# A written-out instruction plan, refitted with measured durations of VectorE, ScalarE and the first GpSimd transfer

## The chip, the core and the metric

The kernel runs on one core of a Trainium2 chip. The metric is the device time of one execution in microseconds. The kernel before takes 267.25 us (median of three runs, 267.24 to 267.47). The profiled execution took 267.04 us; its span, from the first to the last instruction of the program, is 265.3 us, and all times of the profile count from the start of that span.

## What is computed

Sparse attention, and behind it a feed-forward block with a squared relu. Queries, keys and values have 4 batches, 8 heads, 768 rows and 64 columns. The keys are cut into 24 chunks of 32. For each query an upper bound of its score with each chunk comes from the chunk's smallest and largest key in each column; the six chunks with the largest bounds, among those not in the future, are kept.

```python
k_min = np.min(k_chunks, axis=3)
k_max = np.max(k_chunks, axis=3)
ub = np.sum(np.maximum(q[:, :, :, None, :] * k_min[:, :, None, :, :], q[:, :, :, None, :] * k_max[:, :, None, :, :]), axis=-1)
...
top_chunks = np.argsort(ub, axis=-1)[..., -top_k:]
...
scores = np.where(mask, scores, -1000000000.0)
...
attn = np.exp(scores)
attn = attn / (np.sum(attn, axis=-1, keepdims=True) + 1e-09)
return np.matmul(attn, v).astype(np.float32)
...
h = np.maximum(x @ w_in, 0.0)
return (h * h @ w_out).astype(np.float32)
```

The feed-forward block has 3072 tokens, 512 columns and an inner width of 2048.

## The kernel before

**Tiling.** Rows are cut into tiles of 128, six for each batch. The first tile of each batch attends only to itself and needs no selection; it has a path of its own (`first_transposes` L541, `first_attention` L554). The other five tiles of a batch are done for two heads at a time: 16 pairs p = 0 to 15, four for each batch. `stage_a` (L620) prepares a pair: it transposes keys and queries (kT, qT), reduces the keys to the chunks' largest and smallest (kr, L688), forms the positive and negative part of the queries (qp, qm, L704), multiplies for the bounds (ub, L654), adds the causal mask (ubm, L713), finds the top six with max (m8, L662) and compares (selb, L718). The transposed selection is copied into 24 extra rows of the queries (qsc), and the extra rows of the keys hold a large negative number, so that one matmul gives scores with the selection already in them. `stage_b` (L757) computes for each head five banks of scores (ps, L773), the exps on ScalarE (e, L795), a triangular mask on the diagonal blocks (`causal`, L747: on VectorE as a product with tri, L750, or on GpSimd as an affine select, L753) and the product with the values (av, L784). `normalise` (L599) divides by the row sum.

**Feed-forward.** `ffn` (L814) is called once for the four first tiles together and once for the five other tiles of each batch. It transposes x (xt, xT), multiplies with w_in (ph, `up`, L857), takes the relu (ht, on ScalarE L864 or VectorE L866), squares it on VectorE (h, L875), and multiplies with w_out (py, `down`, L888); a copy (ob, L274 or L276) and a store follow.

**Transfers.** GpSimd issues most loads (L361, L439, L446, L426 and the weights, L453 and L459), which turn float32 into bf16. SyncE issues four loads of first tiles (L391), the transposes by DMA of batches 2 and 3 (L381) and the stores.

**The plan.** None of the orders is written by hand. Every operation is a `plan.op` with a cost on each engine that could do it, a due time, and what it needs. `Plan.order` (L112) plays these operations through: it keeps a time at which each engine is free, times at which each buffer comes free, and a small model of the transfers (`Transfers`, L42), always starts what can start first, and among what can start at about the same time on one engine takes the least due time (L157). Where two engines can do an operation, the one that could start it first gets it. `write` (L192) then emits the instructions in the order of these start times. So the costs and due times decide both the order on each engine and which engine does a mask, a copy or a relu. When TensorE is expected to be idle early on, `keep_warm` (L517) fills the gap with matmuls on a constant tile, which no one reads.

The due times come from the table `P` (L234): `lead` says how long before its pair's scores each preparation is due, `va` and `vm` how long after the scores the value product and the mask are due, `f_due` when the first tiles' attention is due, `up_due`, `up_rate`, `due` and `rate` when the feed-forward steps are due, `ra` and `h2` when relu and square are due, `loads` and `later` the order of the transfers.

Of the kernel before, what the change touches and what calls it, by code (L numbers as in the profile page):

```python
# [13 lines left out]
ACT = mybir.ActivationFunctionType  # L14
# [27 lines left out]
class Transfers:  # L42


    RATE = 1 / 0.00083
    FIRST = 600

    def __init__(self):
        self.now = 0.0
# [17 lines left out]
    def add(self, op):  # L67
# [3 lines left out]
        if not op.turns and not self.begun:  # L71
            self.begun = True
            work += self.FIRST
        self.queues[op.turns].append([op, work])
# [3 lines left out]
class Plan:  # L78
# [7 lines left out]
    HAND_OVER = {"PE": 0.22, "ACT": 0.10, "DVE": 0.10, "POOL": 0.12, "SP": 0.1}  # L86
    BUSY = 0.09
    WARM = 8.0
    FILL = 26.0
    NEVER = 1e9  # L90

# [6 lines left out]

    def op(self, where, due, fn, needs=(), tiles=(), packets=0, turns=False,
           late=0.0):  # L100
        op = Op(where, due, fn, [n for n in needs if n is not None],
                [t for t in tiles if t is not None], packets, turns)
        for t in op.tiles:
            t.users.append(op)
        op.late = late
        op.number = -1 if packets and not turns else len(self.ops) - len(self.loads)
        self.ops.append(op)
        if packets and not turns:
            self.loads.append(op)
        return op  # L110

    def order(self):  # L112
        free = {e: 0.7 for e in ("PE", "ACT", "DVE", "POOL", "SP")}
        slots = {tag: [0.0] * n for tag, n in self.slots.items()}
        waiting = {}
        count = {}
        for op in self.ops:
            for t in op.tiles:
                t.left = len(t.users)
            count[op] = len(op.needs)  # L120
            for n in op.needs:
                waiting.setdefault(n, []).append(op)
        ready = [op for op in self.ops if not count[op]]
        landed, done = [], []
        dma = Transfers()
        while ready:
            found = []
            for op in ready:
                if op.packets and not op.turns and op is not self.loads[len(landed)]:
                    continue  # L130
                at = 0.0
                new = {}
                for t in op.tiles:
                    if not t.held:
                        new[t.tag] = new.get(t.tag, 0) + 1
                for tag, n in new.items():
                    at = max(at, sorted(slots[tag])[n - 1]
                             if n <= len(slots[tag]) else self.NEVER)
                if at == self.NEVER:
                    continue  # L140
                if op.packets and not op.turns and len(landed) >= 8:
                    at = max(at, landed[-8].end)
                for engine, cost in op.where.items():
                    st = max(at, free[engine])
                    for n in op.needs:
                        same = n.engine == engine and not n.packets
                        lag = (0.0 if engine == "PE" else self.BUSY) if same                             else self.HAND_OVER[n.engine]
                        st = max(st, n.end + lag)
                    for t in op.tiles:
                        if t.psum:  # L150
                            for e, end in t.last.items():
                                if e != engine and "PE" not in (e, engine):
                                    st = max(st, end + self.HAND_OVER[e])
                    found.append((st, op, engine, cost))
            assert found, "nothing can start"
            first = min(found, key=lambda f: (f[0], f[1].number))
            st, op, engine, cost = min(  # L157
                (f for f in found if f[2] == first[2] and f[0] <= first[0] + self.wait),
                key=lambda f: (f[1].due, f[0], f[1].number))
            ready.remove(op)  # L160
            if engine == "PE":
                op.fill = 0
                fresh = [t for t in op.tiles if t.psum]
                if st < self.FILL and fresh and not any(t.held for t in fresh):
                    room = max([free[engine]] + [sorted(slots[t.tag])[0] for t in fresh])
                    op.fill = max(0, int((st - room - 0.3) / 0.216))
                if st < self.WARM:
                    cost *= 2
            op.engine, op.start, op.end = engine, st, st + cost
            free[engine] = op.end  # L170
            if op.packets:
                dma.add(op)
                if not op.turns:
                    landed.append(op)
            for t in op.tiles:
                if not t.held:
                    t.held = True
                    slots[t.tag].remove(min(slots[t.tag]))
                t.last[engine] = max(t.last.get(engine, 0.0), op.end)
                t.left -= 1  # L180
                if not t.left:
                    slots[t.tag].append(
                        max(u.end + self.HAND_OVER[u.engine] for u in t.users))
            for n in waiting.get(op, ()):
                count[n] -= 1
                if not count[n]:
                    ready.append(n)
            done.append(op)
        assert len(done) == len(self.ops), "operations left"
        return sorted(done, key=lambda op: op.start)  # L190
# [12 lines left out]
def kernel(  # L203
# [27 lines left out]
    QC = 128 * NS  # L231
    VW = 80
    NSET = 4
    P = dict(lead=[26, 15, 48, 47, 26, 61, 5, 53, 70, 14, 26, 79, 70, 28, 8, 54],  # L234
             f_due=[207, -206, -290.97, -438.97], sp='K0 Q0 K1 Q1', rows=-1719,
             rows_after=0, up_due=-34.03, up_rate=11.93, half=4,
             due=[-21, -128, -27, -2], rate=[4.44, 7.05, 5.27, 4.28], va=11.75,
             vm=13.01, ra=0.57, h2=-0.91, later='k1 q1 v1 k2 q2 q3 v2 k3 v3', shift={},
             p0=-7210, wait=0.01,
             loads="k0 q0 V2 Q3 V1 K3 K2 V0 Q2 k1 V3 "  # L240
                   "i0 q1 v0 i3 i2 v1 k2 R2 q2 i1 o0 q3 k3 o1 v2 v3 o2 o3")

    nc.scalar.preload_act_table_set("natural_log_exp_and_others")

# [15 lines left out]
                 "vn": B - 1, "x": 2, "xT": 2,  # L260
                 "kr": 2, "qp": 2, "qm": 2, "ubm": 2, "m8": 2, "rc": 2}, lambda *a: keep_warm(*a), P["wait"])
    POOLS = {"tp": pst, "ps": pss, "av": psav, "ff": psf, "e": epool, "h2": hpool,
# [148 lines left out]
    def ones(b, due):  # L411
        def go(engine):
            e = nc.vector if engine == "DVE" else nc.gpsimd
            e.memset(nat["v", b].tile[:, :, :, D:D + 1].rearrange(
                "p j h o -> p (j h) o"), 1.0)

        made["ones", b] = plan.op({"DVE": 0.12, "POOL": 0.3}, due, go,
                                  tiles=[nat["v", b]])
# [52 lines left out]

    for i, what in enumerate(P["sp"].split()):
        if what[0].isupper():
# [8 lines left out]
    made["ubmask"] = plan.op({"DVE": 0.8}, -997, make_ubmask)  # L482
    for what in P["loads"].split():
        i = int(what[1])
# [11 lines left out]
    for b in range(1, B):  # L496
        ones(b, 20 * NP * b - 70)
    for what in P["later"].split():
        nm, b = what[0], int(what[1])
# [17 lines left out]
    def keep_warm(dst, n):  # L517

        size = 1
        for dim in dst.shape[1:]:  # L520
            size *= dim
        dst = dst if len(dst.shape) == 2 else dst.rearrange(
            {3: "p a b -> p (a b)", 4: "p a b c -> p (a b c)"}[len(dst.shape)])
        if dst.dtype == F32:
            size = min(size, 512) // 128 * 128 or size
            for _ in range(n * 512 // size):
                nc.tensor.matmul(
                    dst[:, 0:size].rearrange("p (a b) -> p a b", b=min(size, 128)),
                    lhsT=warm, rhs=warm[:, 0:min(size, 128)].unsqueeze(1).to_broadcast(
                        [128, size // min(size, 128), min(size, 128)]),  # L530
                    start=True, stop=True)
        else:
            for _ in range(4 * n):
                transpose(dst[:, 0:128], warm)
# [19 lines left out]
    def first_attention(b, tags, due):  # L554
# [30 lines left out]
        for hh in range(2):  # L585
# [5 lines left out]
                        [es[hh], av[hh]])  # L591
            if (b, hh) == (0, P["rows_after"]):
                rows([e])
# [15 lines left out]
    def rows(after):  # L609
        made["rows", 0] = plan.op({"ACT": 0.84}, P["rows"], lambda _: kq_rows(0),  # L610
                                  [made["ident"]] + after)
# [297 lines left out]
    for b in range(B):  # L909
        due = P["f_due"][b]  # L910
# [74 lines left out]
```

The softmax here doesn't subtract the row's maximum and nothing guards it: scores larger than these inputs give would overflow.

## Time and profile before

| engine | busy us | share of 265.3 us | instructions |
|---|---|---|---|
| TensorE, matmuls | 252.9 | 95% | 2378 |
| TensorE, weight loads | 163.9 | 62% | 2403 |
| VectorE | 198.0 | 75% | 699 |
| ScalarE | 180.0 | 68% | 366 |
| GpSimd | 102.9 | 39% | 177 |

A row of a group names the line, the engine, the operation and what it writes and reads, then how often it occurs, its busy time and the mean duration of one in ns, then the idle time of the engine just ahead of it and what ended that. A row of waits names who waited for whom, the sum of these waits, how many there were and the longest. Engines are PE (TensorE), PEld (its weight loads), DVE (VectorE), ACT (ScalarE), POOL (GpSimd) and SP (SyncE). The time of a matmul's row runs from its start to a modelled end, so that rows of matmuls that follow closely overlap.

In 40 slices of the span, TensorE's busy share is 0.9 or more from the seventh slice on to the last but one; VectorE's is 0.9 in most slices between 13 and 150 us and falls off after 210 us; the granted TensorE clock is below full speed only in the first slices.

### The profile page before, as it was taken

Reading aid. Unit: us, or ns where it says so; the run is one execution under the profiler, and the core shown is the slowest. Engines: PE = TensorE matmul, PEld = TensorE weight load, DVE = VectorE, ACT = ScalarE, POOL = GpSimd, SP = SyncE. Lnnn points to the kernel's source line nnn. Section 1 sums busy time; section 2 is a strip of 40 time slices with the busy share of each in tenths; the row PEclk is TensorE's granted clock in tenths of the full one; section 3 lists DMA queues with packets and bytes.
Section 4 is the critical chain, followed back from the end, with each engine's and each line's share of the span. In section 5 each row is a group of like instructions: output and inputs, shape, how many; then the busy total and the mean of one; then the engine's idle time right before and its main releaser. Section 6 shows DMA issues by size and latency. Waiting matters only on the chain.

```text
span 265.3 us, 6528 instructions
## 1 busy us (share of the span) xinstructions
PE 252.9 (95%) x2378; PEld 163.9 (62%) x2403; DVE 198.0 (75%) x699; ACT 180.0 (68%) x366; POOL 102.9 (39%) x177
## 2 busy tenths in 40 slices
PE   6789989999999999999999999999999999999995
PEld 2556755666677666566686556567766666465443
DVE  6689999978999999999998898677877543255000
ACT  1779669855599898769697949667889532376112
POOL 8997756887404837757340112011101000000000
PEclk9689999999999999999999999999999999999999
DMA  9999999999982999999990010263000020200222
GB/s 142 167 177 184 173 171 121 163 155 200 186 138 40 94 129 114 162 140 141 114 249 4 0 53 5 68 129 96 17 0 2 1 80 1 79 4 0 79 82 79
DMA packets 103733, 26.12 MB, mean 98 GB/s; under 512 B 96332, under 2 KB 100708, under 8 KB 103700
## 3 DMA queue, kind: packets, MB, share of 16 engines
q0 software_dynamic: 75168, 13.33, 66.3%
q1 hardware_dynamic: 28532, 12.36, 21.6%
q8 instruction: 19, 0.31, 0.5%
q14 instruction: 14, 0.11, 0.2%
HBM read 27.26 MB, written 6.29 MB: 126 GB/s over the span
## 4 chain that ended last, share of the span: by engine, by line
PE 74%; DVE 11%; ACT 6%; POOL 3%; DMA 2%; issue 2%; SPq 1%; ACTq 0%; DVEq 0%
PE py L888 27%; PE ph L857 25%; PE ps L773 10%; PE av L784 6%; DMA raw<-in_q_dram 2%; DVE h L875 2%; ACT qsc L274 2%; POOL vn L439 2%; DVE kr L688 1%; ACT ht L864 1%; DVE qsc L276 1%; DVE m L662 1%; DVE kqc L276 1%; PE xt L279 1%; PE T L279 1%
## 5 line engine op out<-in xcount | busy, mean ns | idle before, releaser
L857 PE MATMUL ph<-xT,w_in_sb 128*128 128x256 bf16 (+2 forms) x592 | 96.4, 304 | 2.1 <-ACT ht L864 1.2
L795 ACT ACTIVATE e<-ps 128x512 bf16<-128x512 f32 x160 | 87.0, 608 | 9.7 <-PE ps L773 7.4
L888 PE MATMUL py<-w_out_sb,h 128*128 128x512 bf16 (+2 forms) x375 | 88.8, 370 | 1.2
L857 PEld LDWEIGHTS <-w_in_sb 128*128 128x128 bf16 x592 | 56.2, 97 | 27.1 <-issue 4.5
L864 ACT ACTIVATE ht<-ph 128x384 bf16<-128x384 f32 (+2 forms) x120 | 53.6, 452 | 19.5 <-PE ph L857 15.9
L753 POOL TENSOR_SCALAR_AFFINE_SELECT e<-e 128x128 bf16<-128x128 bf16 (+1 forms) x82 | 27.8, 342 | 93.9 <-ACT e L795 84.9
L875 DVE TENSOR_TENSOR h<-ht 128x256 bf16<-128x256 bf16 (+2 forms) x148 | 46.8, 330 | 19.9 <-ACT ht L864 13.1
L888 PEld LDWEIGHTS <-h 128*128 128x128 bf16 x400 | 36.0, 97 | 32.2
L773 PE MATMUL ps<-qsc,kqc 88*128 88x128 bf16 (+1 forms) x320 | 53.2, 272 | 0.1
L274 ACT COPY ob<-py 128x512 f32<-128x512 f32 (+2 forms) x23 | 13.1, 569 | 41.4 <-PE py L888 41.4
L784 PEld LDWEIGHTS <-e 128*128 128x128 bf16 x640 | 33.5, 97 | 10.4 <-POOL e L753 0.5
L784 PE MATMUL av<-vn,e 128*128 128x65 bf16 x480 | 34.2, 193 | 0.1
L773 PEld LDWEIGHTS <-kqc 88*128 88x128 bf16 x320 | 25.5, 97 | 10.0 <-issue 0.4
L604 DVE TENSOR_TENSOR x<-av,rc 128x320 bf16<-128x320 f32 (+1 forms) x40 | 18.8, 472 | 0.5
L750 DVE TENSOR_TENSOR e<-e,tri 128x128 bf16<-128x128 bf16 (+1 forms) x46 | 10.3, 232 | 8.1 <-ACT e L795 7.4
L662 DVE MAX8 m<-ubm 128x8 f32<-128x24 f32 x160 | 15.6, 167 | 0.1
L688 DVE TENSOR_REDUCE kr<-kt 128x24 bf16<-128x768 bf16 x16 | 14.9, 945 | 0.1
L688 DVE TENSOR_REDUCE kr<-kT 128x24 bf16<-128x768 bf16 x16 | 14.8, 949 | 0.1
L784 PE MATMUL av<-v,e 128*128 128x65 bf16 x160 | 14.6, 193 | 0.0
L866 DVE TENSOR_SCALAR ht<-ph 128x256 bf16<-128x256 f32 (+2 forms) x28 | 13.3, 480 | 1.5 <-PE ph L857 1.1
L439 POOL DMA_DIRECT2D vn<-in_v_dram x15 | 13.2, 891 | 0.5 <-issue 0.5
L274 ACT COPY qsc<-sT 24x256 bf16<-24x256 bf16 (+1 forms) x29 | 12.5, 432 | 1.1 <-PE sT L279 0.5
(89 smaller groups left out, 247.7 us busy)
## 6 DMA issues: line engine op xcount, KB each, us to landing
out_dram<-ob SPq DMA_DIRECT2D x23, 256.0 KB, 2.4
w_in_sb<-in_moe_w_in_dram POOLq DMA_DIRECT2D x4, 512.0 KB, 7.7
w_out_sb<-in_moe_w_out_dram POOLq DMA_DIRECT2D x4, 512.0 KB, 8.8
vn<-in_v_dram POOLq DMA_DIRECT2D x15, 128.0 KB, 7.0
nt<-in_k_dram POOLq DMA_DIRECT2D x10, 128.0 KB, 6.1
nt<-in_q_dram POOLq DMA_DIRECT2D x10, 128.0 KB, 5.0
kn<-in_k_dram POOLq DMA_DIRECT2D x8, 80.0 KB, 6.6
qn<-in_q_dram POOLq DMA_DIRECT2D x8, 80.0 KB, 7.1
```

What stands on the lines that cost most here:

```text
L274: nc.scalar.copy(dst, src)
L439: load((nm, b), lambda _: nc.gpsimd.dma_start(out=nat[nm, b].tile[:, j - 1, :, 0:D], in_=SRC[nm][b, :, 128 * j:128 * (j + 1)].rearrange("h ...
L604: return plan.op({"DVE": 0.06 + 0.00108 * D * n}, due, lambda _: nc.vector.tensor_mul(x(), av[:, :, 0:D], rc[:, 0:n].unsqueeze(2).to_broad ...
L688: nc.vector.tensor_reduce(kr[:, mm].rearrange("d (t c) -> d t c", c=128 // CH) if b >= BY_DMA else kr[:, mm], part(kT).rearrange("d t (c j ...
L753: nc.gpsimd.affine_select(out=e, in_=e, compare_op=ALU.is_ge, fill=0.0, base=0, channel_multiplier=-1, pattern=[[0, n], [1, 128]])
L773: nc.tensor.matmul(ps[:, 128 * c:128 * (c + nt)], lhsT=kqs[:, s, hh, 128 * j:128 * (j + 1)], rhs=qss[:, s, hh, 128 * (t0 - 1):128 * (t0 - ...
L784: nc.tensor.matmul(av[:, t - 1], lhsT=e[:, 128 * c:128 * (c + 1)], rhs=value_tile(b, h, j), start=(i == 0 and c == 0), stop=(i == len(BANK ...
L795: nc.scalar.activation(e.tile, ps.tile, ACT.Exp, scale=scale), [sc], [ps, e])
L857: nc.tensor.matmul(ph.tile, lhsT=w_in_sb[:, ki, 128 * f:128 * (f + 1)], rhs=xT[:, c0 // 128:c1 // 128, ki], start=(ki == 0), stop=(ki == N ...
L864: nc.scalar.activation(ht.tile, ph.tile, ACT.Relu)
L875: {"DVE": 0.067 + w / 1920}, at[0] + P["h2"], lambda _: nc.vector.tensor_mul(h2[f][:, c0:c1], ht.tile, ht.tile), [op], [ht, h2[f]])))
L888: nc.tensor.matmul(py.tile, lhsT=h2[f][:, 128 * t:128 * (t + 1)], rhs=w_out_sb[:, f, c0:c1], start=(f == 0), stop=(f == NFI - 1))
```

## The change

The planner's durations are made longer, to what was measured, and all orders are fitted again to the new durations. Four edits do it: the first GpSimd transfer costs 1400 packets more than its size instead of 600 (`FIRST`); each cost on ScalarE is multiplied by 1.04 and each on VectorE by 1.05 (`SLOWER`); due times that are equal up to rounding count as equal, so that the earlier start decides; and the table `P` is replaced. No operation of the computation, no buffer and no matmul shape is changed.

```diff
     RATE = 1 / 0.00083
-    FIRST = 600
+    FIRST = 1400
...
     WARM = 8.0
+    SLOWER = {"ACT": 1.04, "DVE": 1.05}
...
            late=0.0):
+        where = {e: c * self.SLOWER.get(e, 1.0) for e, c in where.items()}
         op = Op(where, due, fn, [n for n in needs if n is not None],
...
-                key=lambda f: (f[1].due, f[0], f[1].number))
+                key=lambda f: (round(f[1].due, 6), f[0], f[1].number))
...
-    P = dict(lead=[26, 15, 48, 47, 26, 61, 5, 53, 70, 14, 26, 79, 70, 28, 8, 54],
-             f_due=[207, -206, -290.97, -438.97], sp='K0 Q0 K1 Q1', rows=-1719,
-             rows_after=0, up_due=-34.03, up_rate=11.93, half=4,
-             due=[-21, -128, -27, -2], rate=[4.44, 7.05, 5.27, 4.28], va=11.75,
-             vm=13.01, ra=0.57, h2=-0.91, later='k1 q1 v1 k2 q2 q3 v2 k3 v3', shift={},
-             p0=-7210, wait=0.01,
-             loads="k0 q0 V2 Q3 V1 K3 K2 V0 Q2 k1 V3 "
-                   "i0 q1 v0 i3 i2 v1 k2 R2 q2 i1 o0 q3 k3 o1 v2 v3 o2 o3")
+    P = dict(lead=[29, 46, 59, 39, 24, 71, 13, 53, 78, 15, 28, 72, 60, 6, 47, 77],
+             f_due=[165, -158, -474.97, -240.97], sp='K0 Q0 K1 Q1', rows=-1719,
+             rows_after=0, up_due=-70.08, up_rate=7.25, half=4,
+             due=[-19, -136, -15, 35], rate=[4.42, 7.43, 6.24, 5.06], va=12.05,
+             vm=6.24, ra=0.55, h2=-1.49, later='k1 q1 v1 k2 q2 q3 v2 v3 k3', shift={},
+             p0=-3220, wait=0.01,
+             loads="Q3 k0 K3 q0 V0 V1 V2 K2 Q2 k1 i0 "
+                   "V3 i3 q1 v0 i2 k2 v1 R2 q2 i1 v2 o0 q3 k3 o1 v3 o2 o3")
```

In `loads`, a capital letter with a batch is the first tile of that batch, a small letter with a number is a pair of heads of batch 0, i and o are quarters of w_in and w_out, and R2 copies the extra key rows to the other sets.

## The prediction

> **What bounds the kernel now.** I read the page first, then the windows, the waits and the groups by shape. The page's first part says that no engine but TensorE is near full over the whole span:
>
> ```profile
> PE 252.9 (95%) x2378; PEld 163.9 (62%) x2403; DVE 198.0 (75%) x699; ACT 180.0 (68%) x366; POOL 102.9 (39%) x177
> ```
>
> An average over 265 us hides the stages, so I cut the span at the first up matmul (22.5 us), where VectorE stops being full (about 152), and at the last matmul (261). The columns are stretch, its length, then the busy time of each engine (its instructions):
>
> ```profile
> core 0: us, PE busy (x) PEld busy (x) DVE busy (x) ACT busy (x) POOL busy (x), PEclk, DMA share, GB/s
> 0.00:22.50 22.50, 17.09 (x171) 10.79 (x172) 16.88 (x66) 13.39 (x24) 20.45 (x31) 0.85 1.74 161
> 22.50:152.00 129.50, 126.24 (x1300) 84.60 (x1311) 121.51 (x426) 102.47 (x211) 72.96 (x119) 1.00 1.38 134
> 152.00:261.00 109.00, 108.29 (x894) 67.56 (x905) 59.60 (x209) 63.34 (x132) 9.52 (x28) 1.00 0.15 45
> 261.00:265.30 4.30, 1.28 (x19) 0.98 (x16) 0.00 (x0) 0.74 (x2) 0.00 (x0) 1.00 0.18 62
> ```
>
> TensorE looks full in both long stages, but a busy matmul row includes its latency. I therefore counted columns: each weight load of the trace is paired with its matmul in the program's order, and a column costs 1/2.4 ns (two 512-column matmuls of the last stage start 216 ns apart, 1% more than this rate). That gives 10.6, 119.2, 105.8 and 0.9 us of streaming in the four stretches, 236.5 us in all. So 11.9 us are lost in the start, 10.3 in the middle, 3.2 in the third stage and 3.4 in the tail. The third stage streams 97% of its time; the middle streams 92%, and there VectorE is busy 121.5 of 129.5 us (94%), ScalarE 79%, GpSimd 56%. In the middle two engines are nearly full together, and neither has room to wait for the other. Who waits for whom over the whole run:
>
> ```profile
> POOL e L753 <- ACT e L795: 84.9, 69, 9.3
> ...
> ACT ht L864 <- PE ph L857: 15.9, 44, 1.5
> DVE h L875 <- ACT ht L864: 13.1, 35, 1.6
> ...
> DVE e L750 <- ACT e L795: 7.4, 17, 1.3
> ...
> PEld L784 <- POOL e L753: 0.5, 2, 0.3
> ```
>
> GpSimd's masks wait for exps far more than anything waits for GpSimd: its 82 masks are held up 84.9 us in total, while the value matmuls (L784) waited 0.5 us for them. Here GpSimd is a spare engine for masks and VectorE is not.
>
> **What the Trainium skill says.** "Perfetto Trace Analysis", Identifying the Most-Contended Engine: matmul busy share is no measure of the distance to the limit, occupancy is a fair one for VectorE. The trace agrees: 126 us busy against 119 streamed. "TensorE: Matmul & The Clock Gate", Part 1: the clock falls to half after an idle window of about 3.4 us and returns after a busy one; its Part 4 says that transposes do not count as busy in the same way. The trace shows clock 0.50 from 8.2 to 15.0 us, two such windows, with mostly transposes in the first. "SBUF — State Buffer", Who interferes with whom: VectorE instructions with two SBUF inputs and GpSimd ones that read SBUF block each other. GpSimd's masks took 282 to 1093 ns with a median of 292, so here this is rare.
>
> **The change part by part.** No matmul of the result, no exp and no transfer is added or taken away; the planner (L112) only gets other costs, and it puts the same operations on other engines and places. Comparing the built orders by engine gives this.
>
> 1. Masks: the 128x128 masks on VectorE (L750) fall from 38 to 18, on GpSimd (L753) they rise from 58 to 78. Of the first 32 masks of pairs 0 to 3, VectorE had 25 and gets 9.
>
> ```profile
> L750 DVE TENSOR_TENSOR e<-e,tri 128x128 bf16<-128x128 bf16 x38 | 8.1, 221 | 7.0 <-ACT e L795 6.5
> L753 POOL TENSOR_SCALAR_AFFINE_SELECT e<-e 128x128 bf16<-128x128 bf16 x58 | 17.4, 302 | 75.5 <-ACT e L795 66.5 <-DVE h L875 8.7
> ```
>
> A mask costs VectorE 0.14 us (start to start with no gap) to 0.22 (its mean row), so 20 of them are 2.8 to 4.4 us less. GpSimd gets 20 x 0.30 = 6.0 us more; its idle time hides that, if the masks do not stand behind transfers.
>
> 2. Copies, at start-to-start durations of back-to-back instructions: VectorE loses 3 key copies (3 x 0.45), 3 long selection copies (3 x 0.36), one t copy (0.34), two relus (0.47 and 0.60): 3.8 us. It gains 4 query copies (4 x 0.43), one ob (0.60), one xT (0.34) and a memset (0.09): 2.7 us. Net 1.1 us less. ScalarE: +3 x 0.73, +3 x 0.48, -4 x 0.67, relus +0.9, the rest cancels: about 1.8 us more, on an engine with 27 us free in the middle. Costed at nothing.
>
> With part 1, VectorE has 3.9 to 5.5 us less to do. Placing each VectorE operation at the matmul that it follows, the work that belongs to the first 130 us of streaming falls by nearly 6 us, since some moves later; that stretch is start and middle.
>
> 3. Order of matmuls. Placed on the streaming axis, the first up group stands at 10.5 us in both orders, the first scores of pair 1 at 22.9 and now 22.3, the first scores of pair 9 at 109.8 and 110.7. No block moves between stages. Value matmuls move back: those of pair 0 end at 25.2 instead of 17.2, those of pair 9 at 136.7 instead of 123.9. That gives a mask on GpSimd time; the six e buffers limit it.
>
> 4. Start. Filler grows: 12 transposes, one 512-column and four 128-column matmuls more, two 256-column ones fewer, 0.86 us of streaming. It lies in the 11.9 us lost there. GpSimd now issues Q3 first, so the two k0 transfers come one issue later; they landed 5.3 to 5.6 us after issue (7.1 and 8.5 us), and one 1024-packet transfer ahead of them at the shared rate of then (640 packets in 1.35 us) puts the second at 8.5 + 1024 x 1.35/640 = 10.6 at the latest, which TensorE's order makes harmless. Walking on with the trace's durations: the Q1 cast ends at 10.1 as before; T of Q1, T of Q3, one filler (0.43 each at half clock) and two presets (0.85) stand ahead of kT, which ends near 12.9 instead of 9.9. On VectorE two kr (0.87 each), two kqc (0.46), kbd, two rc, one x, qp and qm follow, to 17.4; bounds run at 17.5 instead of 15.0. Then ubm, ten max, two x, the selection: its transpose at 20.4 instead of 18.0. Two copies, now on VectorE (0.36 + 0.28), instead of ScalarE: first scores near 21.4 instead of 20.4. But before, the two b=2 exps on ScalarE (21.0 to 22.1) blocked the queue, and the first up ran at 22.5. In the new order those exps end near 22.0 and xT is there at 22.3. The start loses 1 us on the selection and gets it back: 0, bounded by -0.5 and +1.5 (the upper end if the half clock lasts one more window, in which some 3 us of matmuls would take 1.5 more).
>
> 5. Third stage and tail: same work, 3.2 and 3.4 us lost, nothing queued anew: 0.
>
> Sum: I let half of VectorE's relief arrive in the middle, since TensorE is the other full engine. Half of the mean of 3.9 and 6 is 2.5 us; of the 10.3 lost there, 7.8 stay. I take off 0.3 for a few exposed masks. 267.25 - 2.5 + 0.3 = 265.0.
>
> **The rivals.**
>
> All of the relief arrives, and the start gains. VectorE at 94% is then the true bound of the middle: -5 us there, near 262.3. For it: where VectorE has slack (210 us on) streaming is above 97%. Against it: with VectorE at 94%, TensorE would have to stream 96% of a stage full of cross-engine waits.
>
> TensorE's own dependencies bound the middle. Bubbles between scores, exps and values stay whatever VectorE does: 267.3. For it: TensorE's named waits after 30 us are all short, up to 0.7 us. Against it: the loss falls mainly where VectorE is fullest.
>
> Slower: the masks on GpSimd become the wait. GpSimd runs in order; in pairs 0 to 3 its queue holds transfer issues of 0.87 us each, and 16 more masks stand among them. With half an issue ahead of each, they are late by 16 x 0.43 = 7 us in total. The value matmul waits in order on TensorE, with all matmuls behind it; the exps wait for its e buffer. If half is exposed, +3.5, and with 1.7 of the relief kept, +1.8: 269.0. A mask waiting for its exp also holds back the issues behind it. For it: GpSimd was already busy 9 of 10 us around 50 us. Against it: value matmuls stand later, and transfers land 6 to 8 us after issue, so a late issue often costs nothing.
>
> **How the numbers follow.** Main case 0.42 (265.0), full relief 0.24 (262.3), nothing 0.10 (267.3), slower 0.24 (269.0). The range leaves out the far ends of the second and the last: 261.8 to 269.2. Within 0.2% (0.53 us) I put 0.09, faster 0.67, slower 0.24.
>
> **What would show it.** Right: between the first up group and about 150 us, VectorE busy near 117 us and the stage about 2.5 us shorter; the value matmuls' wait for L753 stays below 2 us; the first up starts within 1 us of 22.5. Wrong: TensorE waiting for GpSimd's masks or for w_in, w_out and v transfers; clock 0.50 beyond 15 us; or a middle of the same length with VectorE idle instead of full.

## The result and the profile after

The changed kernel takes 265.99 us (median of four runs, 264.97 to 266.11), against 267.25 us before (267.15 to 267.47). The ratio is 0.9943, with a 95% interval of 0.9918 to 0.9969. Run again beside other kernels it was 265.41 us, ratio 0.9938 (0.9915 to 0.9962). So it is faster by 0.6%, 1.3 to 1.6 us. The prediction said 265.0.

The page's first part, and the same four stretches as before (stretch, its length, busy time and instructions of each engine, clock, share and rate of the transfers):

```profile
PE 252.1 (95%) x2418; PEld 164.5 (62%) x2418; DVE 193.3 (73%) x677; ACT 179.9 (68%) x369; POOL 109.2 (41%) x196
```

```profile
0.00:22.50 22.50, 15.08 (x160) 10.01 (x161) 14.03 (x61) 12.29 (x20) 19.42 (x30) 0.92 1.61 162
22.50:152.00 129.50, 127.96 (x1348) 86.86 (x1346) 121.73 (x424) 105.88 (x223) 79.33 (x136) 1.00 1.38 134
152.00:261.00 109.00, 108.65 (x913) 67.44 (x911) 57.50 (x194) 61.49 (x128) 10.49 (x31) 1.00 0.14 45
261.00:264.40 3.40, 0.36 (x7) 0.19 (x4) 0.00 (x0) 0.30 (x2) 0.00 (x0) 1.00 0.22 77
```

VectorE has 4.7 us less to do over the span (198.0 before). But in the middle, where the prediction looked for about 117 us, it is as busy as it was: 121.73 against 121.51 us. What it lacks is missing in the start (14.03 against 16.88) and in the third stage (57.50 against 59.60). These are stretches of time, and a faster kernel does more in the same time: TensorE is busy 127.96 us in the middle, against 126.24. Cut at equal work, as in the table below, VectorE's busy time in the middle falls from 123.4 to 121.0 us, and to 119.9 when run again, which is 94% of a shorter stage.

The masks and the waits over the whole run:

```profile
L752 DVE TENSOR_TENSOR e<-e,tri 128x128 bf16<-128x128 bf16 x18 | 3.9, 223 | 3.6 <-ACT e L797 3.6
L755 POOL TENSOR_SCALAR_AFFINE_SELECT e<-e 128x128 bf16<-128x128 bf16 x78 | 25.5, 335 | 76.3 <-ACT e L797 67.5 <-DVE h L877 8.8
```

```profile
POOL e L755 <- ACT e L797: 79.1, 62, 8.3
...
DVE h L877 <- ACT ht L866: 14.1, 34, 1.6
ACT ht L866 <- PE ph L859: 14.0, 40, 1.5
...
DVE e L752 <- ACT e L797: 4.3, 7, 1.3
...
PEld L786 <- POOL e L755: 0.9, 4, 0.3
```

The 20 masks did move, and the value matmuls wait 0.9 us for GpSimd's masks, not much more than the 0.5 of before. Lines have moved down by two.

**Where the time went.** I count as the prediction did: each weight load of the trace is paired with its matmul, and a column counts 1/2.4 ns of useful work; a matmul of 48 columns counts as one of 64, and fillers do not count. Then two kernels can be compared at the same amount of useful work. The first 9 us of it are the start, those from 9 to 130 the middle (it ends near 154 us), the rest is the third stage and the tail. Times are from the profiled execution of each kernel; the last four columns are waits of TensorE in the middle, summed over all weight loads that begin more than 0.1 us later than the streaming allows. "FFN" is the product with w_in (ph), "prep" a pair's preparation (kT, qT, ub, sT), "values" av, "scores" ps.

| kernel | start | middle | rest | FFN | prep | values | scores |
|---|---|---|---|---|---|---|---|
| before | 22.75 | 131.38 | 111.21 | 4.33 | 2.56 | 0.55 | 0.22 |
| after | 23.79 | 128.78 | 111.83 | 3.06 | 0.83 | 0.39 | 0.38 |
| after, run again | 23.39 | 127.94 | 111.82 | 2.32 | 0.57 | 0.27 | 0.38 |

The middle is 2.6 to 3.4 us shorter. The start gives back 0.6 to 1.0 of that and the third stage with the tail 0.6. That makes -0.9 in the first profile and -2.2 in the second, around the -1.3 and -1.6 of the medians.

### The profile page after: what moved, and what is told of

Read it like the earlier page. It is cut to its first block, busy times and chain, and to the rows that moved or that the text cites. A ratio compares the mean times of both kernels' runs of the same rounds, so it can differ in the third digit from the quotient of the medians.

```text
span 264.4 us, 6590 instructions
## 1 busy us (share of the span) xinstructions
PE 252.1 (95%) x2418; PEld 164.5 (62%) x2418; DVE 193.3 (73%) x677; ACT 179.9 (68%) x369; POOL 109.2 (41%) x196
## 4 chain that ended last, share of the span: by engine, by line
PE 83%; DVE 6%; ACT 5%; DMA 3%; issue 1%; SPq 0%; POOL 0%; ACTq 0%; DVEq 0%; POOLq 0%
PE py L890 30%; PE ph L859 29%; PE ps L775 12%; PE av L786 7%; DMA raw<-in_k_dram 3%; DVE kr L690 2%; ACT ht L866 2%; ACT qsc L276 1%; PE T L281 1%; DVE kqc L278 1%; PE xt L281 1%; DVE h L877 1%; ACT e L797 1%; PE ub L658 1%; PE qT L281 1%
## 5 line engine op out<-in xcount | busy, mean ns | idle before, releaser
L859 PE MATMUL ph<-xT,w_in_sb 128*128 128x256 bf16 (+2 forms) x592 | 98.0, 304 | 1.6 <-ACT ht L866 1.4
L890 PE MATMUL py<-w_out_sb,h 128*128 128x512 bf16 (+2 forms) x400 | 91.8, 371 | 0.0
L755 POOL TENSOR_SCALAR_AFFINE_SELECT e<-e 128x128 bf16<-128x128 bf16 (+1 forms) x102 | 35.1, 356 | 88.2 <-ACT e L797 79.1
L866 ACT ACTIVATE ht<-ph 128x256 bf16<-128x256 f32 (+2 forms) x122 | 54.8, 455 | 17.6 <-PE ph L859 14.0
L775 PE MATMUL ps<-qsc,kqc 88*128 88x128 bf16 (+1 forms) x320 | 54.4, 272 | 0.8 <-DVE qsc L278 0.7
L786 PEld LDWEIGHTS <-e 128*128 128x128 bf16 x640 | 31.8, 97 | 7.9 <-POOL e L755 0.9
L775 PEld LDWEIGHTS <-kqc 88*128 88x128 bf16 x320 | 27.0, 98 | 12.8 <-issue 1.0
L786 PE MATMUL av<-vn,e 128*128 128x65 bf16 x480 | 32.1, 193 | 0.2 <-POOL e L755 0.2
L276 ACT COPY qsc<-sT 24x384 bf16<-24x384 bf16 (+1 forms) x32 | 14.1, 440 | 1.7 <-DVE qsc L278 1.0
L868 DVE TENSOR_SCALAR ht<-ph 128x256 bf16<-128x256 f32 (+2 forms) x26 | 12.2, 469 | 3.7 <-PE ph L859 3.6
L441 POOL DMA_DIRECT2D vn<-in_v_dram x15 | 13.3, 902 | 1.1 <-DMA kn<-in_k_dram 1.1
L278 DVE COPY qsc<-sT 24x256 bf16<-24x256 bf16 (+1 forms) x32 | 9.6, 301 | 1.7 <-PE sT L281 1.0
```

What stands on the lines that cost most here:

```text
L276: nc.scalar.copy(dst, src)
L755: nc.gpsimd.affine_select(out=e, in_=e, compare_op=ALU.is_ge, fill=0.0, base=0, channel_multiplier=-1, pattern=[[0, n], [1, 128]])
L775: nc.tensor.matmul(ps[:, 128 * c:128 * (c + nt)], lhsT=kqs[:, s, hh, 128 * j:128 * (j + 1)], rhs=qss[:, s, hh, 128 * (t0 - 1):128 * (t0 - ...
L786: nc.tensor.matmul(av[:, t - 1], lhsT=e[:, 128 * c:128 * (c + 1)], rhs=value_tile(b, h, j), start=(i == 0 and c == 0), stop=(i == len(BANK ...
L859: nc.tensor.matmul(ph.tile, lhsT=w_in_sb[:, ki, 128 * f:128 * (f + 1)], rhs=xT[:, c0 // 128:c1 // 128, ki], start=(ki == 0), stop=(ki == N ...
L866: nc.scalar.activation(ht.tile, ph.tile, ACT.Relu)
```

## The experiments

All ratios are to the kernel before, run on the same chip beside each kernel.

**Order and masks, each without the other.** In the first kernel everything is placed as in the changed one, only each mask goes to the engine that it has before:

```diff
+MASK_ON = ('DDDD-PDDD-DDPP-PPDD-PDDD-DDDP-DDDD-DDDD-' ...
-            op.fn(op.engine)
+            at = getattr(op, "mask", None)
+            op.fn(op.engine if at is None else {"D": "DVE", "P": "POOL"}[MASK_ON[at]])
```

> The new order of all instructions, but each of the 128 masks on the engine that it had in the kernel before (46 on VectorE instead of 26). Theory A (relief of VectorE by the masks is what shortens the middle): the 4 us of masks come back on an engine that is 94% full there, the middle loses most of what it gained, 267.0 us or more. Rival B (the gain comes from the order of matmuls and preparations, GpSimd merely takes masks that would have been hidden): 266.0 within 0.4 us. In both, the first up matmul starts as in the new kernel, since no mask runs before it.

Measured: ratio 1.0041 (1.0019 to 1.0064), 267.78 us. The second kernel is the reverse, the old order with the masks on the new engines (the same edit to the kernel before, with the other list):

> The old order of all instructions, but each mask on the engine that the new plan gives it. Theory A: the middle shortens by 1 us or more, 265.7 to 266.3 us. Rival B: no gain without the new order, 267.2 within 0.4. Rival C (masks on GpSimd stand behind transfer issues where the order was not made for it): TensorE waits for L753, 268 or more.

Measured: ratio 1.0135 (1.0122 to 1.0148), 270.64 us. Here GpSimd's masks become what TensorE waits for. Its waits between 22.5 and 152 us:

```profile
PE av L791 <- POOL e L760: 2.1, 3, 1.0
...
PEld L791 <- POOL e L760: 2.6, 4, 1.1
```

VectorE's busy time in this stretch did fall, from 121.5 to 117.6 us, the number that the prediction had named as the sign of success, and the kernel got 3.6 us slower. (Part of the fall is only that a slower kernel does less in the same time; over the span VectorE has 2.2 us less, 195.8.) In the first kernel too TensorE waited for masks, on both engines:

```profile
PE av L793 <- POOL e L762: 0.8, 1, 0.8
PE av L793 <- DVE e L759: 0.3, 1, 0.3
...
PEld L793 <- POOL e L762: 1.5, 3, 1.1
PEld L793 <- DVE e L759: 1.1, 2, 0.8
```

So a mask's engine and the place of its value matmul belong together; one without the other costs. I read the first run as support for VectorE's relief. That was too quick: the loss there lies in value matmuls that wait for masks, and neither run says what VectorE's load as such is worth. What they do say stands in the other waits, counted as in the table above:

| kernel | middle | FFN | prep | values | scores |
|---|---|---|---|---|---|
| new order, masks as before | 130.61 | 2.31 | 0.96 | 3.02 | 0.38 |
| old order, masks as after | 134.26 | 4.19 | 2.33 | 3.62 | 0.22 |

The waits at the FFN and at the preparations go with the order of everything else, whichever engine has the masks; those at the values come from the masks.

**The measured factors alone.** The kernel before with its old table, and only the new factors:

```diff
+    SLOWER = {"ACT": 1.04, "DVE": 1.05}
...
+        where = {e: c * self.SLOWER.get(e, 1.0) for e, c in where.items()}
```

> The kernel before with its old table of due times, only the factors 1.04 and 1.05 on the planner's durations added; its plan then puts some 17 masks more on GpSimd. Theory A: most of the gain of the middle comes with it, about 266.3. Rival B (the due times must be refitted): 267.3 or more.

Measured: ratio 0.9999 (0.9991 to 1.0007), 266.98 us: no change, and less than the rival's 267.3. The plan moved only 4 masks to GpSimd (86 there instead of 82), not 17, so that the run says little about masks. The waits for a pair's preparation fall from 2.56 to 0.96 us, but scores now wait 2.20 (0.22). The gain needs the new table.

**VectorE's masks left out.** In the changed kernel, the masks that VectorE still does are left out:

```diff
         if engine == "DVE":
-            nc.vector.tensor_mul(
-                e, e, tri.unsqueeze(1).to_broadcast([128, n, 128]))
+            pass
```

> The changed kernel with the 26 masks that VectorE still does left out (those on GpSimd stay), so that the attention output is without them: 5.9 us of VectorE work go, of which some 4.5 before 152 us. It measures what VectorE's time in the middle is worth at the end. Theory A (VectorE bounds the middle, full rate): 4 us or more less, 262 us or lower. Half rate, as the prediction took it: 2 to 3 us less, 263 to 264, ratio 0.984 to 0.988. Rival (TensorE's own order bounds it now): less than 0.7 us, above 265.3.

Measured: ratio 0.9945 (0.9925 to 0.9965), 265.39 us. The changed kernel itself, run again, had 0.9938: no difference. Then the same edit to the kernel before, where it takes away 46 masks:

> The kernel before with the 46 masks that VectorE does left out (those on GpSimd stay), so that the attention output is without them: some 10 us of VectorE work go, order of all else unchanged, and no mask is slower than before. It is the same edit as in the changed kernel's run without VectorE's masks, which moved the time by half a microsecond or less. Theory A2 (VectorE bounded the middle of the kernel before, with TensorE's idle time there, 3.3 us, as the ceiling of what relief can bring; the changed kernel has used up about half of it and is now bound by TensorE): 263.5 to 265.3 us, ratio 0.987 to 0.993, and TensorE's busy time between 22.5 and 152 us rises from 126.2 to 127.5 or more. Rival (TensorE's own order bound the kernel before as well, and the gain came from the order alone): above 266.3, ratio over 0.997.

Measured: ratio 0.9989 (0.9979 to 1.0000), 266.72 us. The middle stretch of both, first the kernel before without VectorE's masks, then the changed one:

```profile
22.50:152.00 129.50, 126.61 (x1306) 84.86 (x1316) 117.95 (x399) 102.95 (x212) 72.38 (x119) 1.00 1.35 134
```

```profile
22.50:152.00 129.50, 127.78 (x1330) 86.64 (x1341) 119.60 (x414) 106.11 (x222) 78.08 (x134) 1.00 1.39 134
```

VectorE has 8.0 us less to do over the span of the first (190.0 against 198.0), more relief than the change gives, and about 0.3 us of it arrives (0 to 0.6 by the interval). At equal work VectorE is busy 119.4 us in the middle of the first, less than in the changed kernel (121.0 and 119.9), and this middle still takes 130.9 us, against 128.8 and 127.9. So VectorE's load of masks bounded neither kernel. And with no mask on VectorE in either, the new order still beats the old by 1.3 us (265.39 against 266.72). The gain is in the other work: its order, and the engines of its copies and relus, which the new table sets together. What TensorE waits for in the middle stays where it was, first the kernel before, then the same without VectorE's masks:

```profile
PEld L857 <- issue: 4.3, 13, 0.7
PEld L279 <- issue: 0.9, 2, 0.7
PEld L279 <- DVE selb L718: 0.9, 4, 0.3
PEld L654 <- DVE kbd L695: 0.6, 1, 0.6
```

```profile
PEld L856 <- issue: 4.2, 13, 0.5
PEld L279 <- issue: 1.1, 3, 0.6
PEld L279 <- DVE selb L718: 0.6, 3, 0.3
PEld L654 <- DVE kbd L695: 0.5, 1, 0.5
```

and in the changed kernel, run again:

```profile
PEld L859 <- issue: 1.7, 4, 0.8
...
PEld L281 <- DVE kr L690: 0.4, 1, 0.4
PEld L786 <- POOL e L755: 0.4, 2, 0.2
PEld L281 <- issue: 0.3, 1, 0.3
```

The row that I passed over was L857's "issue": 13 weight loads of the product with w_in, 4.3 us. The timeline of before shows what one is:

```profile
72.73 0.69 ACT L274 COPY qsc<-qT 64x640 bf16<-64x640 bf16 x1
...
73.45 0.38 ACT L864 ACTIVATE ht<-ph 128x256 bf16<-128x256 f32 x1
...
73.88 0.49 PE L857 MATMUL ph<-xT,w_in_sb 128*128 128x256 bf16 x3 [0.28 <-ACT ht L864]
```

There are two PSUM tiles for ph. The product at 73.88 needs the one that the relu at 73.45 frees, and this relu stands behind a 0.69 us copy of a pair's queries in ScalarE's queue. TensorE's next instruction waits, and all behind it. Not every wait is of this kind. Of the 15 that make the 4.33 us of "FFN" in the table, 12 end with a relu on ScalarE (3.3 us), seven of these right behind a copy onto qsc (2.2 us), and three with a relu on VectorE (1.0 us). The waits of a pair's preparation end nearly all with an operation of VectorE (kr, selb, kbd), so that the place of these operations in VectorE's queue counts, though its load of masks does not.

**Exchanges in TensorE's order alone.** If these waits are all, putting a ready block of scores ahead of a waiting instruction should fill them. The kernel before, with ten such exchanges by hand:

```diff
+MOVED = [(195, 314), (409, 373), (477, 435), (753, 749), (757, 753),
+         (578, 698), (599, 786), (605, 891), (1128, 1289), (1132, 994)]
...
+        for what, behind in MOVED:
+            op = self.ops[what]
+            todo.remove(op)
+            todo.insert(1 + todo.index(self.ops[behind]), op)
```

> The kernel before with every mask, copy and relu on the engine and in the place it had; only ten pieces of TensorE's order are exchanged by hand with a neighbour, at places where the trace of before shows TensorE's next instruction waiting (an FFN product for a PSUM tile that a relu has to free, or the turning of a pair's queries) while a block of scores that was ready stood right behind it. The waits at these ten places sum to about 2.4 us, of which two thirds might be filled. Theory B (what the change gains comes from the order of TensorE's queue, whose head waits less often for ScalarE's relus and for a pair's preparation; VectorE's load of masks has nothing to do with it): TensorE's time lost to such waits in the middle falls by 0.7 to 1.6 us and the time by as much, 265.4 to 266.3 us, ratio 0.994 to 0.9975. Rival (the waits come back at the next instruction, since ScalarE and VectorE have as much to do as before): 266.8 or more, ratio over 0.9985.

Measured: ratio 1.0016 (1.0007 to 1.0025), 267.54 us. The rival holds. The waits came back one place on, now also at scores (L781):

```profile
PE ph L865 <- DVE ht L874: 0.9, 1, 0.9
PE ph L865 <- ACT ht L872: 0.9, 3, 0.4
PE ps L781 <- ACT qsc L282: 0.5, 1, 0.5
PE ps L781 <- ACT e L803: 0.5, 1, 0.5
```

Waits of the FFN fell to 3.30 us and of the preparation to 1.40, those of scores rose to 1.74 and of values to 0.88; the middle took 131.61 us instead of 131.38. (The profiled execution took 268.30 us; of what it lost, 1.0 us was lost in the start, ahead of the first exchange.) At these places ScalarE and VectorE have as much to do as before in the same time. This points to how relus, copies and preparations are spread over those queues. It does not show it: only these ten exchanges were tried, no relu or copy was moved by itself, and which entries of the new table make the gain was not separated.

**The start.** First the fillers of the changed kernel left out (`if op.fill:` becomes `if False:`):

> The new kernel without its filler matmuls in the start (24 transposes of a constant, one 512-column and four 128-column matmuls); nothing that is read is left out. The new kernel had the half clock for one window of 3.4 us (8.8 to 12.2), the old one for two (8.2 to 15.0). Theory D (the longer filler ends the half clock early and saves some of the start): two windows again, first up 0.5 to 1.5 us later, 266.5 to 267.5. Rival E (the start waits for transfers, casts and VectorE, the clock costs nothing there): 266.0 within 0.4, whatever the clock shows.

Measured: ratio 0.9966 (0.9956 to 0.9977), 266.22 us. The clock was at half from 8.6 to 22.2 us instead of 8.8 to 12.2 and the first FFN product ran at 23.80 us instead of 22.92. The start took 24.67 us, 0.9 more than after. The first product is later by what theory D said, with four windows at half speed instead of its two; the time is that of rival E. The interval overlaps those of the changed kernel (265.99 and 265.41 us), so that the fillers' worth can't be told.

Then pair 0's keys put back to the front by hand:

```diff
+MOVED = [(15, 17), (277, 144), (280, 277), (281, 9), (278, 281), (282, 174), (279, 174)]
```

> The changed kernel with its start put back by hand and everything else left as planned: the two loads of pair 0's keys (k0) are issued on GpSimd ahead of the first transfer of Q3, TensorE turns pair 0's keys as soon as the copy of K1 has freed their PSUM tile, and VectorE's four operations on them (two maxima kr, two copies kqc) come right behind that copy instead of behind two first copies. Theory A (the gain was halved because VectorE lost 2.85 us of busy time in the first 22.5 us, which then had to be done in the middle stage, which VectorE bounds): the first kr starts at 10 to 11 us instead of 13.3, the first scores come at or before 21.2 instead of 22.2, VectorE's busy time between 22.5 and 152 us falls below 120.5 (121.7), and the time is 264.3 to 265.3 us, 0.989 to 0.993 of before. Theory B (the start's delay was made up by 40 us and costs nothing at the end): the start moves in the same way, but the time stays at 265.8 to 266.3, ratio 0.995 to 0.997. Theory C (the first attention now comes behind the keys, so the first FFN matmul is later than 23.5): 266.5 or more.

Measured: ratio 0.9976 (0.9957 to 0.9994), 266.26 us. The first kr did start at 10.80 us instead of 13.30. But the first attention now came behind it, and the first FFN product ran at 25.44 us: theory C's sign, with a time at the upper end of theory B's. Theory A's was missed. The profiled execution is the slowest of the 22 (268.64 us), with the clock at half from 8.6 to 15.4 and from 18.8 to 22.2 us, so that its start says more about the order than about the median.

Only the two loads of those keys ahead of Q3 (the first exchange of the line above):

> The changed kernel with one move: the loads of pair 0's keys are issued ahead of the first transfer of Q3 on GpSimd; all orders on TensorE, VectorE and ScalarE stay. It tells the transfers' share of the late start from the order's. If the late start comes from GpSimd's first transfer taking the DMA engines from SyncE's load of K1 (landed at 8.8 us, 7.3 before), K1 lands no sooner by this, since the bytes are the same, and Q3 lands at about 11.2 instead of 8.3, behind which TensorE's filler and its transposes stand: first kr no earlier than 13, time 265.8 to 266.8. If it is the order of the loads alone that delays the keys: first kr at 11.5 to 12, first scores 0.8 us sooner, time 265 to 265.5.

Measured: ratio 0.9931 (0.9910 to 0.9951), 265.12 us. K1 landed at 7.87 us, though in the profiles of the changed order it lands anywhere from 7.2 to 8.8, and the first kr started at 12.78, between the two cases. In the changed kernel run again it started at 11.54 with no move at all, so that one profile's start can't tell these cases apart. The time is that of the second case, but the changed kernel run again had 0.9938, so this move is worth nothing that can be told. The same move with 20 more filler transposes ahead of those of K1:

> The changed kernel with pair 0's keys issued ahead of Q3, and 20 more filler transposes on TensorE ahead of the transposes of K1, where it idles for 1.4 to 2.4 us at about 7 us. In the changed order each half-speed window of 3.4 us near the start went with a longer time (263.9 without one, about 265.3 with one, 266 to 267 with two), in the order before not. If TensorE bounds the changed kernel, so that its clock in the start now counts, and if the filler keeps the clock up: mean clock 0.994 to 1.0, time 264 to 264.8, ratio 0.989 to 0.992. If the filler does not raise the clock, or only delays the transposes of K1: 265.1 or more, as without it.

Measured: ratio 0.9938 (0.9914 to 0.9961), 265.66 us. The half-speed window was not taken away but came later, from 16.2 to 19.6 us, in the place where it also was in the changed kernel run again (15.9 to 19.3). No gain; and its one run without a half-speed window took 266.29 us, so that the count of such windows, from which the expectation was made, does not order the times.

**The end, and the changed kernel again.** The old lead for the last three pairs (`60, 6, 47, 77]` becomes `60, 28, 8, 54]`):

> The changed kernel with the old lead for its last three pairs only (28, 8, 54 instead of 6, 47, 77: how far ahead of its scores a pair is prepared). The changed kernel was 1.2 to 1.5 us ahead of the one before at the same amount of matmul work up to 150 us and only 0.6 to 0.9 ahead from 165 us on. If the new leads of the last pairs give that back: 265.0 to 265.5 us, ratio 0.992 to 0.994. If it is given back because the last pairs' stage is bound by TensorE in both kernels, or by ScalarE's exponentials: unchanged, 265.8 to 266.3. If the new leads fit the new order better: 266.5 or more.

Measured: ratio 0.9957 (0.9930 to 0.9985), 265.72 us. It can't be told from the changed kernel, and its rest took 112.22 us, 0.4 more: the leads of the last pairs are not what gives back in the third stage.

> The changed kernel itself again, beside the others on this chip, to have its spread under the same conditions: 265.5 to 266.2 us, ratio 0.993 to 0.997. If its median is within 0.3 us of that with pair 0's keys issued first (265.1), that one move is worth nothing that can be measured.

Measured: ratio 0.9938 (0.9915 to 0.9962), 265.41 us, 0.1 below the expected range and 0.3 above the run with pair 0's keys issued first. None of these versions beats the changed kernel by more than the intervals.

## Why the prediction was right in its number and wrong in its reason

**The bound of the middle.** The step that failed is the reading "In the middle two engines are nearly full together", and with it the term of the sum made from it, half of VectorE's relief. VectorE was busy 94% there. The Trainium skill, "Perfetto Trace Analysis", Identifying the Most-Contended Engine, calls occupancy a fair measure for VectorE, and I took it for a bound. The runs disagree with that: 8.0 us less on VectorE moved the kernel before by 0.3 us. TensorE lost its time at the head of its own queue, to the FFN's products (4.33 us, most of it behind relus on ScalarE) and to the steps of a pair's preparation (2.56 us). Without VectorE's masks both are nearly as long, 4.2 and 2.2 us.

**Parts 1 and 2, masks and copies.** The counts came as read from the orders, and VectorE's busy time fell by 4.7 us, within the 3.9 to 6 given. As a gain the masks are worth no more than the 0.3 us (0 to 0.6) of the run without them. The copies were costed at nothing on ScalarE; what their new engines are worth was not measured by itself.

**Part 3, order of matmuls.** It was taken as the thing that makes room for the masks. That is shown: in the old order the moved masks cost 3.6 us. But the order, with the engines of copies and relus, carries the gain as well. The prediction gave it no gain of its own, and in the waits of the middle it is 1.3 to 2.0 us at the FFN and 1.7 to 2.0 at the preparations.

**The size.** The middle fell by 2.6 to 3.4 us where 2.5 was predicted. This is luck: half of a relief that was worth about 0.3 us happens to be near what the shorter waits gave. The sum is then off by its zeros.

**Part 4, start.** Costed at 0, it measured +0.6 to +1.0. First scores ran at 22.24 us (21.4 predicted, 20.40 before; 21.84 in the second profile), the first FFN product at 22.92 (22.52 before and in the second profile). The second k0 transfer landed at 11.2 us (10.1 in the second profile), later than the 10.6 given as the latest. The walk was near up to the selection: kT ended at about 13.3 us and the selection was turned at 20.52, against 12.9 and 20.4 (11.5 and 19.8 in the second profile). What came after it was later than walked. I had the first scores follow the copies onto qsc on VectorE. In the first profile they did not start when the first two of these were done (21.55), and the profile names VectorE:

```profile
20.91 1.34 DVE L278 COPY qsc<-sT 24x384 bf16<-24x384 bf16 x4 [0.44 <-PE sT L281]
...
22.24 0.38 PE L775 MATMUL ps<-qsc,kqc 88*128 88x256 bf16 x2 [0.71 <-DVE qsc L278]
```

But the last of the four copies ended at 22.25, after the scores had begun. Ahead of them, at 22.19, ended the first of two exps of a first tile, which stood behind two key copies on ScalarE:

```profile
19.95 1.61 ACT L276 COPY kqc<-kT 64x768 bf16<-64x768 bf16 x2
21.59 1.08 ACT L589 ACTIVATE e<-ps 128x512 bf16<-128x512 f32 x2
```

In the second profile the four copies were done at 21.51, and there the profile names the exp, which ended at 21.79:

```profile
PE ps L775 <- ACT e L589: 1.1, 1, 1.1
```

So the first scores waited for this exp, which frees a PSUM tile of scores. The walk had the exps end near 22.0 and put them ahead of the first FFN product only.

The clock was at half in one window in each: 8.8 to 12.2 us in the first profile, 15.9 to 19.3 in the second. In neither did it last longer than before (8.2 to 15.0 us), as the upper bound allowed for.

**Part 5, third stage and tail.** Costed at 0, it measured +0.6. Of that, 0.41 is one value matmul at about 169 us (168 in the second profile); the rest is spread too thin to name.

**The rivals.** "TensorE's own dependencies bound the middle" was right that waits stay when VectorE is relieved of masks. It placed them between scores, exps and values, where only 0.22 and 0.55 us lay; the larger ones are at the FFN and the preparations. Its time, 267.3, was wrong, since the new order has fewer of these waits. "The masks on GpSimd become the wait" is what happens in the old order (270.64 us, 269.0 named). "All of the relief arrives" falls with VectorE as the bound.

**The signs named.** Value matmuls' wait for L755 below 2 us and the first FFN product within 1 us of 22.5: both came. VectorE near 117 us did not, and where it came, in the old order with the masks moved, the kernel was slower. It was no sign of a gain at all. Of the signs of being wrong, the clock at 0.50 beyond 15 us came in the second profile, whose execution was the faster one (264.86 against 266.11 us); it was no sign either.

## What to carry to other kernels

A busy share of 94% does not make an engine the bound. Before a relief is costed, list what the bounding engine's next instruction waits for, with "issue" rows of weight loads among it, and ask which of these waits the moved work releases; or leave the work out and see. In a plan of in-order queues the engine of an operation and the place of its consumer are one choice: here the new order with the masks on their old engines was 0.4% slower than the kernel before, the new engines for the masks alone 1.35% slower, and both together 0.6% faster. And a releaser that the profile names is to be checked against its end: one that ends after the wait did not end it.

## What the runs showed of the hardware that was not expected

The same program ran the middle in 128.78 us in one profile and in 127.94 in the other. Two copies of keys on VectorE, inside SBUF, fall beside five transfer issues on GpSimd. VectorE in the first profile, then GpSimd:

```profile
88.90 1.67 DVE L278 COPY kqc<-kt 64x768 bf16<-64x768 bf16 x2
90.59 1.81 DVE L690 TENSOR_REDUCE kr<-kt 128x24 bf16<-128x768 bf16 x2
```

```profile
86.01 4.38 POOL L428 DMA_DIRECT2D nt<-in_q_dram  x5
```

and in the changed kernel run again:

```profile
88.48 0.97 DVE L278 COPY kqc<-kt 64x768 bf16<-64x768 bf16 x2
89.47 1.81 DVE L690 TENSOR_REDUCE kr<-kt 128x24 bf16<-128x768 bf16 x2
```

```profile
85.60 4.58 POOL L428 DMA_DIRECT2D nt<-in_q_dram  x5
```

One such copy takes 344 to 357 ns where nothing on GpSimd lies beside it, and 797 and 860 ns in the first profile, 337 and 623 in the second; where the copies are slower the issues are faster, 4.38 against 4.58 us. The other profiles that keep this order and its masks fall into the same two kinds. That with pair 0's keys put back has 797 and 860 ns and a middle of 128.79 us. Those without fillers, with pair 0's keys issued first, with these and more fillers, and with the old lead at the end have 329 to 337 and 622 to 625 ns and middles of 127.96 to 128.05 us. The two reductions right behind take 1.81 us in both, though in the second profile the first of them still lies beside the issues. The Trainium skill, "SBUF — State Buffer", Who interferes with whom, says that a copy can enter a mode in which it shares ports with GpSimd, that whoever starts first holds them for the whole instruction, and that reductions do not contend; the trace agrees with the last, and the lengthened copies fit the first. Who started first does not tell the two kinds apart, though: in both, the first copy began 0.28 to 0.29 us after an issue, and then either the copy was the longer one (797 ns beside an issue of 903) or the issue was (1101 ns beside a copy of 337). Behind the longer pair, a transposed selection and an FFN product waited 0.26 and 0.74 us on TensorE, and about as long in the other profile of this kind, but in none of the other kind. That the copies caused this is read from the order of events and was not tested by itself.
